# VectorE's order in a fused convolution and MLP kernel: taps moved behind one PSUM closing, another closing cut in two, one sum moved from GpSimd

## The chip, the core and the metric

The kernel runs on one core of a Trainium2 chip. The metric is the device time in microseconds (us) of one execution, the median of several. The engines of the core are called PE (TensorE: matrix products; PEld is its loading of weights, which overlaps the products), DVE (VectorE), ACT (ScalarE), POOL (GpSimd) and SP (SyncE, used here to start DMAs only). Each works through its own queue in the order in which the program was written, and waits on semaphores for what other engines and DMAs deliver.

## What is computed

The input `x` is 8 x 4224 x 192 floats. The reference does two things, one after the other:

```python
w = softmax(weight)                                   # 8 heads x 7 taps
out[b, s, c] = sum_k w[head(c), k] * x_pad[b, s + k, c]   # causal convolution along s
xn = (out - mean(out)) / sqrt(var(out) + 1e-6) * g_ln      # over the 192 channels
result = out + relu(xn @ w_ch1) @ w_ch2                    # 192 -> 768 -> 192
```

All of it is in float32. The convolved rows are called y below.

## The kernel before

**Tiling.** Rows are cut into 18 groups: three small ones at the start (g0 to g2), then g3 to g17 with 16 rows in each of the 128 partitions. Only the groups from g3 on, the "mixed" ones, matter here. The tiles are laid out by hand, the framework does no scheduling (`tc.manual_schedule()`), so the order of the statements is the order on each engine's queue; the framework adds only the waits.

**One group** goes through these stages. y is made by seven taps for each of 8 heads: tap 0 on ACT (`first_tap`, L384), tap 1 on ACT into a tile `tb` that a DMA started by POOL adds to y (`second_tap`, L395 and L398, "y<-tb"), and taps 2 to 6 on DVE (`conv`, L409, one instruction for a head and a tap). DVE then transposes y in 32x32 blocks to `yt` (L420). The up product is `up_mixed`, the down product `down_fast`. Both are one level of a seven-product block scheme (sums and differences of quarters replace the eighth product). For it, four sums of quarters of `yt`, called s1 to s4, are made by `sums_of_y` (L576 to L579): s1 = a21 + a22, s2 = s1 - a11, s3 = a21 - a11, and s4 in place of a21. The norm is folded in: its scale `rstd` multiplies the result at the end (`scale`, L886, on ACT), and the unscaled y was stored first, so that the scaled result is added to it in DRAM by a DMA (`add_to_out`, L893).

**The up product.** PSUM's eight banks make two sets, X (banks 0 to 3) and Y (banks 4 to 7). `up_mixed` has two passes, `one` and `two`, and each pass has seven products of about 2 us on PE (L519) that go to X and Y in turn. What a product leaves must be taken out before the set's next product but one starts: `evict` copies it with ACT (L617); `close` adds it to what is already there, with DVE (L623) where no spare tile is given, and with an ACT copy into a spare tile and a DMA accumulation (L582) where one is given. In every group but the last, DVE closes exactly two products, both of pass `two`: the **upper left** quarter `two.c11`, out of X after the second product, and the **lower left** quarter `two.c21`, out of X after the sixth. The product that follows the upper left closing in X is the fourth of the pass; what follows the lower left closing in X is the first down product, since `take_bank` hands out banks 0, 1, 2, ... from there. After a closing comes `lower_sum` (L773), a relu joined with a difference.

**The down product.** `down_fast` (L804) runs seven products of three column blocks each. The first one writes bank 0, 2 and 4 in this order. ACT takes each block out (L811) and between blocks does a few items of a list `work`: a relu of `one.c22`, scales of the group before, a relu of `two.c22`, and the first and second tap of the group after the next; `behind` says how many items go after each block. DVE does three sums over halves (`half_sum`, L771), adds to c11 (L836) and to a part (`add_part`, L853), starts the sums of y of the next group (L575 to L579) and takes the moments of its y (L440). DVE's `finish_fast` (L861: three transposes for each half, with an `add_part` ahead of the second half) is called from the next group's `up_mixed`, through the generator `ahead`.

**DVE's order around the change,** in one group: moments, `finish_fast` of the group before in two halves, 16 + 5 taps of the next group (taps 2 and 3, and tap 4 of five heads), upper left closing, 8 taps, `lower_sum` of pass one, lower left closing, `lower_sum` of pass two, 11 taps, transpose of the next y, the half sums.

**The last group** has no next group: DVE does all its closings itself, no taps stand between them, and the multiplication of the group before by `rstd` is done by DVE, in two instructions (L683), after the upper left closing of pass two.

Of the kernel before, what the change touches and what calls it, by code (L numbers as in the profile page):

```python
# [11 lines left out]
ALU = mybir.AluOpType  # L12
# [4 lines left out]
def kernel(  # L17
# [29 lines left out]
    nc = tc.nc  # L47
    PSUM = bass.MemoryType.PSUM
    B, S, D = x.shape
    H, K = weight.shape  # L50
    F = moe_w_ch1.shape[1]
    P = 128
# [10 lines left out]
    NQ = P // C  # L63
# [19 lines left out]
    HJ = J // 2  # L83
# [3 lines left out]
    W = HJ * C  # L87
# [285 lines left out]
    y, yt, rstd = {}, {}, {}  # L373
# [192 lines left out]
    def sums_of_y(g, engine):  # L566

        room = upool.tile([P, 3 * HJ * CH * C], F32, tag="ys", name=f"ysums{g}")
        room = room.rearrange("p (v j c t) -> p v j c t", v=3, c=CH, t=width(g))
        s1, s2, s3 = [room[:, v] for v in range(3)]  # L570
        a11, a12, a21, a22 = quarters_of_y(g)
        ysums[g] = s1, s2, s3, a21
        if engine is not nc.vector:

            nc.vector.memset(s1[:, 0:1, 0:1, 0:1], 0.0)  # L575
        engine.tensor_tensor(s1, a21, a22, op=ALU.add)  # L576
        engine.tensor_tensor(s2, s1, a11, op=ALU.subtract)
        engine.tensor_tensor(s3, a21, a11, op=ALU.subtract)
        engine.tensor_tensor(a21, a12, s2, op=ALU.subtract)  # L579
# [4 lines left out]
    def up_mixed(g, ahead, pending):  # L584


        last = g + 1 == NG
        assert groups[g][2] == 2 * HJ and 3 * W // 2 <= 512 and FC == PAIR + 1
        hidden_tile(g)
        a = ht[g]  # L590
        a11, a12, a21, a22 = quarters_of_y(g)
        b11, b12, b21, b22 = quarters_of_w1()
        t2, t3, t4 = [w1sums[:, k] for k in range(3)]
        s1, s2, s3, s4 = ysums[g]
        done = groups[g - 1][2]
        js = a11.shape[1] // 2

        class Pass:
            def __init__(self, s):
                self.s = s  # L600
                (self.c11, self.c12), (self.c21, self.c22) = [
                    [a[:, h, e, s] for e in range(2)] for h in range(2)
                ]

            def product(self, to, left, right, first=True, end=True):
                s = self.s
                for i, f, ps in (
                    (slice(0, W), s, slice(0, 2 * js)),
                    (slice(W, W + W // 2), PAIR, slice(js * s, js * s + js)),
                ):  # L610
                    rows_of_tiles(
                        to[:, :, i], right[:, :, P * f : P * f + P], left[:, ps], first and i.start == 0, end, True
                    )

            def evict(self, banks, dst, relu=False):
                src = banks[:, :, 0 : W + W // 2]
                nc.scalar.activation(dst, src, AF.Relu) if relu else nc.scalar.copy(dst, src)  # L617

            def close(self, c, banks, part=None):


                if part is None or last:
                    nc.vector.tensor_tensor(c, c, banks[:, :, 0 : W + W // 2], op=ALU.add)  # L623
                    return
                self.evict(banks, part)
                whole = "p q w -> p (q w)"
                add_by_dma(c.rearrange(whole), part.rearrange(whole))

            def relu(self, c):
                nc.scalar.activation(c, c, AF.Relu)  # L630

        def part_of(pool, tag):

            part = pool.tile([P, J * D], F32, tag=tag, name=f"part_{tag}{g}")
            return part[:, 0 : NQ * (W + W // 2)].rearrange("p (q w) -> p q w", q=NQ)

        def act_scales(j1, j2):
            if not last:
                scale(g - 1, j1, j2)

        def taps_of_next(*args, **kw):
            if not last:
                conv(g + 1, *args, **kw)


        X, Y = take_set(), take_set()
        one, two = Pass(0), Pass(1)
        p = one
        p.product(X, a11, b11, True, False)
        p.evict(X, p.c11)  # L650
        p.product(Y, a12, b21)
        p.close(p.c11, Y, two.c12)
        next(pending, None)
        p.product(X, s2, t2, False, False)
        p.evict(X, p.c21)
        p.product(Y, s3, t3, True, False)
        p.evict(Y, p.c22)
        next(ahead)
        p.product(X, s1, b12, False, False)
        p.close(p.c22, X, part_of(cpool, "cs"))  # L660
        next(pending, None)
        p.product(Y, a22, t4, False)
        p.close(p.c21, Y, part_of(bpool, "tb"))
        p.product(X, s4, b22, False)
        p.evict(X, p.c12, True)
        taps_of_next(2, 4)
        taps_of_next(4, 5, heads=(0, 5))

        p = two
        p.product(Y, a11, b11, True, False)  # L670
        p.evict(Y, p.c11)
        p.product(X, a12, b21)
        one.relu(one.c11)
        act_scales(0, 1)
        p.close(p.c11, X)
        taps_of_next(4, 5, heads=(5, H))
        taps_of_next(5, 6, heads=(0, 5))
        lower_sum(g, (0,))
        if last:

            for j1 in (0, HJ):
                part, factor = ots[g - 1][:, j1 : j1 + HJ], rstd[g - 1][:, j1 : j1 + HJ]
                nc.vector.tensor_tensor(  # L683
                    part, part, factor.unsqueeze(2).to_broadcast([P, HJ, D]), op=ALU.mult
                )
                add_to_out(g - 1, j1, j1 + HJ)
        p.product(Y, s2, t2, False, False)
        p.evict(Y, p.c21)
        p.product(X, s3, t3, True, False)
        p.evict(X, p.c22)  # L690
        p.product(Y, s1, b12, False, False)
        p.close(p.c22, Y, part_of(bpool, "tb"))
        p.product(X, a22, t4, False)
        p.relu(p.c11)
        act_scales(1, 2)
        p.close(p.c21, X)
        if last:
            one.relu(one.c22)
            p.relu(p.c22)
        p.product(Y, s4, b22, False)  # L700
        p.evict(Y, p.c12, True)
        lower_sum(g, (1,))
        if last:

            for f in range(FC):
                for s, ws, _ in columns(g, f, fast[g], J):
                    rest = a[:, 1, 0, s, :, ws]
                    nc.scalar.activation(rest, rest, AF.Relu)
        taps_of_next(5, 6, heads=(5, H))
        taps_of_next(6, K)  # L710

        def scale_one(j):
            scale(g - 1, j, j + 1)
            if j == 7:
                add_to_out(g - 1, 0, 8)
            elif j == done - 1:
                add_to_out(g - 1, 8, done)

        if last:
            return []  # L720
        work = [lambda: one.relu(one.c22)]
        work += [lambda j=j: scale_one(j) for j in range(2, done)]
        return work[0:9] + [lambda: two.relu(two.c22)] + work[9:]

    po = {}

# [124 lines left out]
    def add_part(half, cs, parts):  # L851
        fresh = cs[:, CH * half : CH * half + CH, 1]
        nc.vector.tensor_tensor(fresh, fresh, parts[half], op=ALU.add)  # L853

    def finish_fast(g, half, flat, cs, parts):
        n = fast[g]
        ot = ots[g] if half else out_tile(g)
        if half:
            add_part(half, cs, parts)
        for c in range(CH * half, CH * half + CH):  # L860
            nc.vector.transpose(  # L861
                ot[:, 0:n, C * c : C * c + C], flat[:, c].rearrange("p (j t) -> p j t", t=C)
            )
# [11 lines left out]
    ots = {}  # L875
# [12 lines left out]
    def add_to_out(g, j1, j2):  # L888
        if groups[g][0] is None:

            j1, j2 = (0, j2) if j2 == groups[g][2] else (0, 0)
        for ps, rows in rows_of_out(g, j1, j2) if j2 else ():
            nc.gpsimd.dma_start(  # L893
                out=rows, in_=ots[g][ps, j1:j2].rearrange("p j d -> p (j d)"), accum_op=ALU.add
            )
# [53 lines left out]
    results, pending = None, iter(())  # L949

    def ahead(g):


        if results is not None:
            for half in range(2):
                finish_fast(g - 1, half, *results)
        yield

    for g in range(NG):
        mixed, last = g in MIXED, g + 1 == NG  # L960
# [36 lines left out]
            store_y(g + 1)  # L997
        results = down_fast(g, work)
        if last:
            for half in range(2):  # L1000
                finish_fast(g, half, *results)
            add_and_store(g, slice(0, fast[g]))
            down(g)
            finish(g)
        else:
            if g % 2 or g + 2 == NG:
                pending = root(g + 1 - g % 2)
# [30 lines left out]
```

## Time and profile before

Three runs gave 981.8, 982.68 and 982.71 us; the median is 982.68 us. The profiled execution has a span of 980.9 us.

The groups show up as stretches between the first up product of one group and that of the next. A stretch holds the group's up product (14 products) and its down product. The starts come from PE's timeline:

| group | starts at us | length us | | group | starts at us | length us |
|---|---|---|---|---|---|---|
| g3 | 123.27 | 55.47 | | g11 | 574.67 | 58.21 |
| g4 | 178.74 | 55.48 | | g12 | 632.88 | 56.02 |
| g5 | 234.22 | 56.22 | | g13 | 688.90 | 55.63 |
| g6 | 290.44 | 58.28 | | g14 | 744.53 | 56.55 |
| g7 | 348.72 | 56.36 | | g15 | 801.08 | 57.22 |
| g8 | 405.08 | 56.20 | | g16 | 858.30 | 56.63 |
| g9 | 461.28 | 55.80 | | g17 | 914.93 | 66.0 to the end |
| g10 | 517.08 | 57.59 | | | | |

How to read the profile: a group of instructions is named by its line, its engine, its operation and "out<-in". In a timeline each line has the start, the duration, the engine, the line of code and, in square brackets, the idle time of that engine just before and what ended it. "issue" means that nothing in the profile explains the idle time. The down product took 27.4 to 27.5 us in each group from g3 to g16, so what varies in the table lies in the up products.

### The profile page before, as it was taken

Reading aid. Unit: us, or ns where it says so; the run is one execution under the profiler, and the core shown is the slowest. Engines: PE = TensorE matmul, PEld = TensorE weight load, DVE = VectorE, ACT = ScalarE, POOL = GpSimd, SP = SyncE. Lnnn points to the kernel's source line nnn. Section 1 sums busy time; section 2 is a strip of 40 time slices with the busy share of each in tenths; the row PEclk is TensorE's granted clock in tenths of the full one; section 3 lists DMA queues with packets and bytes.
Section 4 is the critical chain, followed back from the end, with each engine's and each line's share of the span. In section 5 each row is a group of like instructions: output and inputs, shape, how many; then the busy total and the mean of one; then the engine's idle time right before and its main releaser. Section 6 shows DMA issues by size and latency. Waiting matters only on the chain.

```text
span 980.9 us, 43680 instructions
## 1 busy us (share of the span) xinstructions
PE 956.8 (98%) x19962; PEld 748.5 (76%) x19962; DVE 906.8 (92%) x1439; ACT 667.2 (68%) x1069; POOL 293.7 (30%) x397
## 2 busy tenths in 40 slices
PE   6999999999999999999999999999999999999997
PEld 5886596877868686786959678695968778596887
DVE  6999999999998999999999899999999999999757
ACT  5625668586776968676786857678695867766351
POOL 2005311714144141534127141441317141261400
PEclk9999999999999999999999999999999999999999
DMA  8243887759495785949587684958868596755031
GB/s 197 96 132 122 178 196 202 156 128 254 100 269 114 214 188 123 240 99 278 119 236 155 157 206 95 276 119 238 165 171 199 101 269 123 182 113 99 3 67 68
DMA packets 24390, 158.14 MB, mean 161 GB/s; under 512 B 3343, under 2 KB 4239, under 8 KB 20110
## 3 DMA queue, kind: packets, MB, share of 16 engines
q0 software_dynamic: 17104, 92.02, 47.9%
q1 hardware_dynamic: 6798, 63.34, 17.5%
q8 instruction: 156, 2.56, 1.0%
q14 instruction: 28, 0.23, 0.1%
q10 hardware_dynamic: 304, 0.00, 0.0%
HBM read 38.95 MB, written 50.33 MB: 91 GB/s over the span
## 4 chain that ended last, share of the span: by engine, by line
PE 71%; ACT 10%; DMA 9%; DVE 8%; issue 2%; POOL 1%; SPq 0%; DVEq 0%; ACTq 0%; POOLq 0%
PE ps L519 36%; PE ps L804 28%; DMA y<-tb 6%; PE ps L745 6%; DVE y L409 6%; ACT ot L886 3%; ACT y L384 2%; ACT tb L395 2%; ACT room L630 1%; ACT cs L811 1%; DVE room L623 1%; DMA xg<-in_x_dram 1%; DMA room<-part_tb 1%; PE ps L321 1%; DMA ga<-in_moe_g_ln_dram 1%
## 5 line engine op out<-in xcount | busy, mean ns | idle before, releaser
L409 DVE SCALAR_TENSOR_TENSOR y<-xg,taps,y 128x384 f32<-128x384 f32 (+3 forms) x734 | 368.7, 579 | 11.7 <-issue 10.7
L519 PE MATMUL ps<-yt,w 32*128 32x256 f32 (+3 forms) x5184 | 239.0, 334 | 4.3 <-issue 3.0
L519 PEld LDWEIGHTS ps<-yt,w 32*128 32x128 f32 x5184 | 220.7, 186 | 23.5 <-issue 11.6
L804 PE MATMUL ps<-room,w2sums 128*32 128x256 f32 (+3 forms) x4416 | 236.5, 371 | 1.4 <-issue 1.4
L617 ACT COPY room<-ps 128x1536 f32<-128x1536 f32 x104 | 149.7, 1439 | 90.4 <-PE ps L519 90.4
L804 PEld LDWEIGHTS ps<-room,w2sums 128*32 128x32 f32 x4416 | 140.7, 110 | 91.7 <-ACT room L630 5.4
L804 PE MATMUL ps<-room,w 128*32 128x256 f32 (+3 forms) x3312 | 180.7, 371 | 0.2 <-issue 0.2
L771 DVE TENSOR_TENSOR room<-room 128x1536 f32<-128x1536 f32 (+1 forms) x96 | 149.0, 1622 | 16.6 <-ACT cs L811 9.7
L804 PEld LDWEIGHTS ps<-room,w 128*32 128x32 f32 x3312 | 104.8, 110 | 65.8 <-DVE room L623 1.8
L519 PE MATMUL ps<-ysums,w1sums 32*128 32x128 f32 (+1 forms) x2880 | 130.1, 325 | 3.8 <-DVE room L623 2.1
L519 PEld LDWEIGHTS ps<-ysums,w1sums 32*128 32x128 f32 x2880 | 120.9, 186 | 10.4 <-DVE room L623 4.1
L811 ACT COPY cs<-ps 128x256 f32<-128x256 f32 (+1 forms) x180 | 65.3, 364 | 47.3 <-PE ps L804 46.9
L886 ACT ACTIVATE ot<-ot,r 128x192 f32<-128x192 f32 x232 | 94.1, 453 | 0.0
L893 POOL DMA_DIRECT2D out_dram<-ot x40 | 34.3, 1087 | 187.5 <-ACT ot L886 160.2
L630 ACT ACTIVATE room<-room 128x1536 f32<-128x1536 f32 x60 | 89.2, 1490 | 0.0
L623 DVE TENSOR_TENSOR room<-room,ps 128x1536 f32<-128x1536 f32 x34 | 59.5, 1752 | 22.4 <-PE ps L519 22.0
L384 ACT ACTIVATE y<-xg,taps 128x384 f32<-128x384 f32 (+3 forms) x141 | 74.0, 604 | 8.5 <-DMA out_dram<-y 6.9
L440 DVE BATCH_NORM_STATS2 st<-y 128x6 f32<-128x192 f32 x264 | 70.3, 348 | 0.0
L582 POOL DMA_DIRECT2D room<-part_tb x28 | 24.2, 865 | 149.2 <-DVE room L773 102.5
L519 PE MATMUL ps<-yt,w1sums 32*128 32x256 f32 (+1 forms) x1440 | 66.3, 323 | 1.2 <-issue 1.2
L519 PE MATMUL ps<-ysums,w 32*128 32x256 f32 (+1 forms) x1440 | 65.9, 323 | 0.6 <-issue 0.6
L811 ACT COPY room<-ps 128x256 f32<-128x256 f32 (+1 forms) x90 | 32.1, 375 | 49.3 <-PE ps L804 49.3
(106 smaller groups left out, 980.4 us busy)
## 6 DMA issues: line engine op xcount, KB each, us to landing
xg<-in_x_dram SPq DMA_DIRECT2D x15, 2112.0 KB, 19.8
out_dram<-ot POOLq DMA_DIRECT2D x29, 768.0 KB, 9.8
y<-tb POOLq DMA_DIRECT2D x28, 768.0 KB, 11.4
room<-part_tb POOLq DMA_DIRECT2D x28, 768.0 KB, 6.3
out_dram<-y SPq DMA_DIRECT2D x13, 1536.0 KB, 10.8
room<-room POOLq DMA_DIRECT2D x14, 768.0 KB, 6.3
room<-part_cs POOLq DMA_DIRECT2D x14, 768.0 KB, 6.3
xg<-in_x_dram SPq DMA_DIRECT2D x1, 1536.0 KB, 7.5
```

What stands on the lines that cost most here:

```text
L384: nc.scalar.mul(y[g][:, 0:n, cs], xg[g][:, 0:n, cs], taps[:, h, 0:1])
L409: nc.vector.scalar_tensor_tensor(out=y[g][:, 0:n, cs], in0=t[:, k : k + n, cs], scalar=taps[:, h, k : k + 1], in1=y[g][:, 0:n, cs], op0=AL ...
L440: nc.vector.bn_stats(out=sums[g][:, j, :], in_=y[g][:, j, :])
L519: nc.tensor.matmul(to[:, q], right[rows, c], left[rows, :, c], skip_group_check=split, start=(first and c == 0), stop=(last and c == left. ...
L617: nc.scalar.activation(dst, src, AF.Relu) if relu else nc.scalar.copy(dst, src)
L623: nc.vector.tensor_tensor(c, c, banks[:, :, 0 : W + W // 2], op=ALU.add)
L630: nc.scalar.activation(c, c, AF.Relu)
L745: nc.tensor.matmul(bank[C * q : C * q + C, 0:w], w2[:, f, C * c : C * c + C], left, start=(f == 0), stop=(f == NF - 1),)
L771: nc.vector.tensor_tensor(d, l, r, op=op)
L804: nc.tensor.matmul(dst[C * q : C * q + C, ws], right[:, f, C * c : C * c + C], view[:, :, q] if len(view.shape) == 4 else view[:, q], star ...
L811: nc.scalar.copy(out[:, c], dst[:, 0:w].rearrange("p (j t) -> p j t", t=t))
L886: nc.scalar.mul(ots[g][:, j, :], ots[g][:, j, :], rstd[g][:, j : j + 1])
```

## The change

It rearranges DVE's queue, with a few moves that go with it:

1. **Fewer taps ahead of the upper left closing.** Of tap 4's five heads that stood ahead of it, three go behind it, so that 18 taps stand ahead and 11 behind, where 21 and 8 stood.
2. **Lower left closing in two pieces.** `close` gets `pieces`; the closing of `two.c21` becomes two instructions, for banks 0 and 1 and for banks 2 and 3. It comes later in the queue by the three taps, and the first piece alone frees the bank that the down product wants first.
3. **First sum of y on DVE.** s1 is made by DVE instead of POOL. A small memset on DVE that held POOL's first sum back until DVE was there goes away.
4. **The relu of `two.c22` in two instructions** on ACT, the columns that are needed first ahead. The list `work` gets one item longer.
5. **`finish_fast` in two steps.** The generator `ahead` yields after the first half and `add_part`; `up_mixed` takes this first step ahead of the closing of `one.c11`. Except in the last group, DVE has no instruction in between, so its order stays.
6. **The last group's output work forward.** The two multiplications by `rstd` and their DMAs go ahead of pass two, from behind its upper left closing.

The diff, cut to its core:

```diff
@@ sums_of_y
-        if engine is not nc.vector:
-            nc.vector.memset(s1[:, 0:1, 0:1, 0:1], 0.0)
-        engine.tensor_tensor(s1, a21, a22, op=ALU.add)
+        nc.vector.tensor_tensor(s1, a21, a22, op=ALU.add)
         engine.tensor_tensor(s2, s1, a11, op=ALU.subtract)
@@ Pass.close
-            def close(self, c, banks, part=None):
+            def close(self, c, banks, part=None, pieces=1):
                 if part is None or last:
-                    nc.vector.tensor_tensor(c, c, banks[:, :, 0 : W + W // 2], op=ALU.add)
+                    for i in range(pieces):
+                        qs = slice(NQ * i // pieces, NQ * (i + 1) // pieces)
+                        nc.vector.tensor_tensor(
+                            c[:, qs], c[:, qs], banks[:, qs, 0 : W + W // 2], op=ALU.add
+                        )
                     return
@@ up_mixed, pass one
         p.product(Y, a12, b21)
+        next(ahead)
         p.close(p.c11, Y, two.c12)
...
         taps_of_next(2, 4)
-        taps_of_next(4, 5, heads=(0, 5))
+        taps_of_next(4, 5, heads=(0, 2))
+
+        if last:
+            for j1 in (0, HJ):
+                part, factor = ots[g - 1][:, j1 : j1 + HJ], rstd[g - 1][:, j1 : j1 + HJ]
+                nc.vector.tensor_tensor(
+                    part, part, factor.unsqueeze(2).to_broadcast([P, HJ, D]), op=ALU.mult
+                )
+                add_to_out(g - 1, j1, j1 + HJ)
@@ up_mixed, pass two
         p.close(p.c11, X)
-        taps_of_next(4, 5, heads=(5, H))
+        taps_of_next(4, 5, heads=(2, H))
         taps_of_next(5, 6, heads=(0, 5))
         lower_sum(g, (0,))
-        if last:
-            for j1 in (0, HJ):
-                part, factor = ots[g - 1][:, j1 : j1 + HJ], rstd[g - 1][:, j1 : j1 + HJ]
-                nc.vector.tensor_tensor(
-                    part, part, factor.unsqueeze(2).to_broadcast([P, HJ, D]), op=ALU.mult
-                )
-                add_to_out(g - 1, j1, j1 + HJ)
...
-        p.close(p.c21, X)
+        p.close(p.c21, X, pieces=2)
@@ the list work
-        return work[0:9] + [lambda: two.relu(two.c22)] + work[9:]
+        halves = [lambda ws=ws: two.relu(two.c22[:, :, ws]) for ws in (slice(W, W + W // 2), slice(0, W))]
+        return work[0:9] + halves + work[9:]
@@ ahead
-            for half in range(2):
-                finish_fast(g - 1, half, *results)
+            flat, cs, parts = results
+            finish_fast(g - 1, 0, flat, cs)
+            add_part(1, cs, parts)
+        yield
+        if results is not None:
+            finish_fast(g - 1, 1, flat, cs)
         yield
```

More of the change, by code (lines that the diff above doesn't have):

```diff
@@ L853, in add_part, with finish_fast @@
         nc.vector.tensor_tensor(fresh, fresh, parts[half], op=ALU.add)
-    def finish_fast(g, half, flat, cs, parts):
+    def finish_fast(g, half, flat, cs):
         n = fast[g]
         ot = ots[g] if half else out_tile(g)
-        if half:
-            add_part(half, cs, parts)
         for c in range(CH * half, CH * half + CH):
@@ L999 @@
         if last:
-            for half in range(2):
-                finish_fast(g, half, *results)
+            flat, cs, parts = results
+            finish_fast(g, 0, flat, cs)
+            add_part(1, cs, parts)
+            finish_fast(g, 1, flat, cs)
             add_and_store(g, slice(0, fast[g]))
```

## The prediction

> **What bounds the kernel.** The page's busy line comes first, then the busy time of each engine by group:
>
> ```profile
> PE 956.8 (98%) x19962; PEld 748.5 (76%) x19962; DVE 906.8 (92%) x1439; ACT 667.2 (68%) x1069; POOL 293.7 (30%) x397
> 178.70:234.20 55.50, 55.50 (x1180) 43.12 (x1176) 53.89 (x80) 41.98 (x66) 23.69 (x33) 1.00 0.70 173
> 290.40:348.70 58.30, 56.72 (x1180) 44.27 (x1176) 53.88 (x80) 41.97 (x66) 22.75 (x33) 1.00 0.72 175
> 348.70:405.10 56.40, 55.54 (x1184) 43.05 (x1180) 53.80 (x81) 41.97 (x66) 14.24 (x13) 1.00 0.75 181
> ```
>
> The last three are g4, g6 and g7: stretch and length, then PE, PEld, DVE, ACT, POOL. PE runs almost without a pause in a good group, so 55.47 us (g3, g4) is nearly PE's own time. DVE has 53.8 us of work in each, 1.7 us less: it is a near second. Over g3 to g16 the lengths exceed 55.47 us by 791.66 - 14 x 55.47 = 15.1 us; that, small gaps inside the good groups and the last group are all that can be gained.
>
> The waits of PE, asked for group by group, split those 15.1 us in two. In g7, g8, g9, g12 and g13 PE waits for DVE's closing, or for nothing that is shown in g3 and g4; their excess is 0.89 + 0.73 + 0.33 + 0.55 + 0.16 = 2.66 us. In g5, g6, g10, g11, g14 and g15 the waits say "issue", in pieces of 0.3 to 0.9 us, between 13 and 26 us after the group's start; excess 0.75 + 2.81 + 2.12 + 2.74 + 1.08 + 1.75 = 11.25 us. g16 has 1.16 us, mostly a wait for ACT behind a DMA. Here is the first kind, DVE and PE in g7:
>
> ```profile
> 367.70 1.75 DVE L623 TENSOR_TENSOR room<-room,ps 128x1536 f32<-128x1536 f32 x1
> 369.37 4.32 DVE L409 SCALAR_TENSOR_TENSOR y<-xg,taps,y 128x384 f32<-128x384 f32 x8
> 373.60 1.76 DVE L773 SCALAR_TENSOR_TENSOR room<-room 128x1536 f32<-128x1536 f32 x1
> 375.82 1.75 DVE L623 TENSOR_TENSOR room<-room,ps 128x1536 f32<-128x1536 f32 x1 [0.47 <-PE ps L519]
> ...
> 369.51 2.24 PE L519 MATMUL ps<-ysums,w1sums 32*128 32x256 f32 x48 [0.86 <-DVE room L623]
> 377.63 4.09 PE L804 MATMUL ps<-room,w 128*32 128x256 f32 x72
> ```
>
> The upper left closing starts at 367.70 straight after the taps, late; PE idles 0.86 us for it. The lower left one waits for PE, so there DVE has time to spare. The chain of waits tells why the first is late:
>
> ```profile
> 379.57 1.39 ACT room L630
> ...
> 397.96 0.54 POOL y L398
> 398.50 12.60 DMA y<-tb
> ...
> 412.78 10.35 DVE y L409 x20
> ...
> 423.99 1.68 DVE room L623
> ```
>
> It is a ring from closing to closing: down product 9.93 us after the closing; ACT's list of relus, scales and taps; the DMA that adds the second tap to y; taps at 412.78, which is 35.15 us after that down product began (377.63); 11.2 us of taps; closing. 9.93 + 35.15 + 11.2 = 56.28 us, and the closings 367.70 and 423.99 are 56.29 us apart. The ring is 0.8 us longer than PE's group. g3 and g4 had slack in hand; from g7 on it sets the pace wherever no "issue" pause has given slack back.
>
> **What the Trainium skill says.** "SBUF — State Buffer", section "SBUF: two separate sides": a DVE instruction with two SBUF inputs and a GpSimd instruction that reads SBUF exclude each other for a whole instruction. The trace agrees: `add_part` takes 0.95 us when POOL is idle, 2.54 us at 292.52, while POOL's last sum runs until 294.25. "Perfetto Trace Analysis", section "Optimizing Scalar/DVE Operations": some 60 ns on SBUF and 125 ns on PSUM are paid for each DVE instruction, and breaking an instruction up can free others sooner. "Runtime: NRT & Kernel Launch", section "Instruction fetch mechanics": instructions come by DMA in blocks of 256. The page has 156 such packets (2.56 MB, 16 KB each); the "issue" pauses of g6 lie 6.1 and 6.2 us apart, and 256 of PE's instructions, half of them products of which 48 go in 1.96 us, are 128 / 48 x 1.96 = 5.2 us, or about 5.9 with a pause of 0.6. So I take those pauses for fetches, an inference. The edits leave PE's instructions alone, so I leave the 11 us.
>
> **The change, part by part.** T is the start of the upper left closing.
>
> *Three taps behind it.* A tap costs 11.2 / 21 = 0.534 us in a row, so DVE comes to the closing 1.6 us earlier. The ring falls to 56.28 - 1.6 = 54.7 us. PE then sets T.
>
> *What they delay.* In g7 DVE goes from 367.70 through closing, 8 taps and `lower_sum` to 375.28, T + 7.58; with three more taps T + 9.18. The lower left closing, which before started when PE was done, now starts when DVE is. Where PE sets T (g4: T = 196.85, the product in X ended near 196.5, the next one needs T + 1.8) the four products after it end at T + 9.76, and the down product began at T + 9.93. Now the first piece decides. The price of a piece has no row: 0.951 us is DVE's own 128x768 sum in SBUF, and between 417 ns for 128x256 out of PSUM (L836) and 1752 ns for 128x1536 (L623) a straight line gives 0.95 for 768 as well; with the page's larger PSUM share 1.0. I take 0.95: piece one ends at T + 10.13, PE begins 0.07 later (the step from 369.45 to 369.51 in g7) at T + 10.2. That is 0.27 us worse than before in a group where PE sets T. The second piece ends at T + 11.05, and the bank it frees is wanted one block after T + 10.2, a third of 3.9 us later: T + 11.5, hidden. Without pieces it would be T + 11.0: they are needed.
>
> Queued behind are `lower_sum` (wanted 3.9 us after the down product began: T + 14.1, it ends T + 12.8, hidden), 11 taps, transpose, then the half sums: they waited 0.52 us for PE and now come some 0.2 us late, with their first use 3.9 us after they start. Hidden.
>
> *The relu in two.* PEld waits 0.4 us for it (ACT L630) in every group, and the second and third down products take 7.88 us where two others take 7.77. The first piece comes half a us sooner: -0.11 us a group. On the ring it costs one more ACT instruction, 0.1 us, and the list is one longer (33 items, 30 go in the first four products, two after the next block), so the last second tap goes behind one more copy, 0.27 us: +0.37 us. Ring: 54.7 + 0.27 + 0.37 = 55.3 us, under PE's group.
>
> *PE's group now:* 55.47 + 0.27 - 0.11 = 55.63 us where PE sets T. In the groups with a pause between T and the down product (g5, g6, g10, g11, g14, g15, g16) DVE has that pause in hand (T + 9.76 plus 0.6 or more), so the pieces remove even the 0.17 us gap: -0.17 - 0.11 = -0.28, of which I take 0.25.
>
> *First sum on DVE.* It adds 0.95 us and takes away 0.06; POOL's three sums end 1.0 us sooner (it began 0.2 us after the memset, now after the sum: 0.95 + 0.2 + 3 x 1.83 against 0.2 + 4 x 1.83), so `add_part`, which lost 1.6 us to the lock, loses none. DVE gains 0.7 us, and its taps wait for the DMA anyway (1.09 us idle before them in the chain). Zero. *`finish_fast` in two:* zero, order unchanged but for g17, where DVE had waited 3.98 us.
>
> *Last group.* 3.42 us of multiplication go into a wait of 4.55 us of DVE ahead of 933.71. The closing of c22 can then start with PE at 939.7, not 940.12; PE had lost 0.42 us there and 0.2 at the down product. Gain 0.5 us. The tail from 966 on is PE and its last output, untouched.
>
> **Sum.** g3, g4, g7, g8, g9, g12, g13: 7 x 0.16 = 1.1 us of excess instead of 2.66, -1.55. Seven groups with a pause: -7 x 0.25 = -1.75. Last group -0.5. Together -3.8: **978.9 us**.
>
> **Rivals.** *A, the lower left closing becomes the bound.* The down product waits for both pieces, or pieces cost well over 1 us. For it: the closing loses its whole slack of 0.47 us, and DVE is 97% busy. Against: each piece has banks of its own. Then PE begins at T + 9.18 + 1.9 + 0.07 = T + 11.15, 1.2 us later than before: 7 x 1.1 - 2.66 for the quiet groups, some 7 x 0.3 for the others, -0.5 at the end: +6.6, 989 us. *B, one wait for another.* The ring goes but each piece costs 0.2 us more than I think, or the DMA of the second tap, issued 0.37 us later, lands later by 1 us. Then 14 x 0.25 = 3.5 of my gain is eaten: 982.4 us. *C, the pauses shrink.* With ring and gaps gone the engines stand otherwise to the DMAs; a third of the 11.25 us of pauses goes: 975.2 us. The same could go the other way; nothing in the profile says which.
>
> **Chances.** Forecast 0.54, A 0.13, B 0.18, C 0.15. The range goes from a little under C to beyond B, with half of the way to A left out: 974.5 to 984.0. Faster by more than 0.2% (under 980.7): the forecast less one in ten, and C: 0.65. Slower (over 984.6): A and a little of the pauses growing: 0.16. The rest, 0.19, lies within.
>
> **What would show it.** In a quiet group (g4, g8): the idle time of PE before its fourth product of pass two ("DVE room L623") at 0.3 us or none, closings 55.6 us apart, DVE idle ahead of the upper left closing for PE, none ahead of the lower left one; a first piece of 0.95 us ending 10.1 us after T and the down product at once; no PEld wait for L630; `add_part` at 0.95 us each time; "issue" pauses in the same groups. I am wrong if the down product starts later than T + 10.5, if the taps still begin so late that PE waits, or if the pauses move.

## The result and the profile after

The changed kernel takes 977.27 us (median of 4 runs, 974.48 to 978.25) where the kernel before takes 982.69; the ratio is 0.9942, 95% interval 0.992 to 0.9965. That is 5.4 us or 0.55% faster. The profiled executions have spans of 974.4 and 980.9 us, 6.5 us apart.

The busy line of the page of the changed kernel, and the busy time of each engine in g4, g6 and g7 (stretch and length, PE, PEld, DVE, ACT, POOL):

```profile
PE 952.9 (98%) x19962; PEld 746.3 (77%) x19962; DVE 897.1 (92%) x1454; ACT 668.4 (69%) x1083; POOL 266.6 (27%) x383
179.40:235.00 55.60, 55.38 (x1180) 43.06 (x1180) 52.98 (x81) 42.06 (x67) 21.37 (x32) 1.00 0.70 172
290.60:348.50 57.90, 56.34 (x1177) 43.90 (x1177) 53.41 (x82) 42.06 (x67) 21.42 (x32) 1.00 0.73 176
348.50:404.20 55.70, 55.48 (x1184) 43.17 (x1180) 52.73 (x80) 42.06 (x67) 12.12 (x12) 1.00 0.76 184
```

g4 and g7 are now alike at 55.6 us, and DVE has about a microsecond less to do in each; g6 is still the long one. The chain that ended last, from the page before and then from the page after, says the same for the whole kernel:

```profile
PE 71%; ACT 10%; DMA 9%; DVE 8%; issue 2%; POOL 1%; SPq 0%; DVEq 0%; ACTq 0%; POOLq 0%
```

```profile
PE 86%; DVE 8%; DMA 2%; issue 2%; POOL 1%; ACT 0%; DVEq 0%; POOLq 0%; ACTq 0%
```

ACT and the DMA of the second tap have left it: the ring from closing to closing no longer sets the pace. Summed over the kernel, PE waited 2.4 us before for DVE's closings inside the up products and shows no such wait after; at the down products it now waits 1.7 us for them, eight times. What took its place stands in the timeline of DVE and PE in g7 of the changed kernel (lines are numbered anew: the closings are L622, `lower_sum` L777, the down product L808):

```profile
356.21 9.62 DVE L409 SCALAR_TENSOR_TENSOR y<-xg,taps,y 128x384 f32<-128x384 f32 x18 [1.84 <-issue]
366.60 1.75 DVE L622 TENSOR_TENSOR room<-room,ps 128x1536 f32<-128x1536 f32 x1 [0.77 <-PE ps L519]
368.27 5.91 DVE L409 SCALAR_TENSOR_TENSOR y<-xg,taps,y 128x384 f32<-128x384 f32 x11
374.09 1.75 DVE L777 SCALAR_TENSOR_TENSOR room<-room 128x1536 f32<-128x1536 f32 x1
375.76 1.81 DVE L622 TENSOR_TENSOR room<-room,ps 128x768 f32<-128x768 f32 x2
...
366.28 4.37 PE L519 MATMUL ps<-ysums,w1sums 32*128 32x256 f32 x96
376.76 4.09 PE L808 MATMUL ps<-room,w 128*32 128x256 f32 x72 [0.21 <-DVE room L622]
```

The wait has changed sides. DVE now stands idle for 0.77 us ahead of the upper left closing, PE has no marked wait there (its two products from 366.28 on run as one row of 4.37 us), and the lower left closing, which had waited 0.47 us for PE, now starts straight after `lower_sum`; PE waits 0.21 us for its first piece.

The lengths by group in us, from PE's timeline:

| group | before | after | change | | group | before | after | change |
|---|---|---|---|---|---|---|---|---|
| g3 | 55.47 | 55.60 | +0.13 | | g10 | 57.59 | 57.19 | -0.40 |
| g4 | 55.48 | 55.60 | +0.12 | | g11 | 58.21 | 58.16 | -0.05 |
| g5 | 56.22 | 55.62 | -0.60 | | g12 | 56.02 | 55.78 | -0.24 |
| g6 | 58.28 | 57.97 | -0.31 | | g13 | 55.63 | 55.60 | -0.03 |
| g7 | 56.36 | 55.60 | -0.76 | | g14 | 56.55 | 56.55 | 0.00 |
| g8 | 56.20 | 55.60 | -0.60 | | g15 | 57.22 | 57.07 | -0.15 |
| g9 | 55.80 | 55.59 | -0.21 | | g16 | 56.63 | 55.88 | -0.75 |

g3 to g16 together: 791.66 before, 787.81 after, -3.85 us. The last group: from 65.97 us (980.9 - 914.93) to 62.88 us (974.4 - 911.52), -3.09 us. What comes before g3 is 0.44 us longer (123.71 against 123.27); another profile of the same changed kernel begins g3 at 126.66, so that part varies by itself. -3.85 - 3.09 + 0.44 = -6.5.

### The profile page after: what moved, and what is told of

It reads as the page before. It is cut to its first block, busy times and chain, and to the rows that moved or that the text cites. A ratio compares the mean times of both kernels' runs of the same rounds, so it can differ in the third digit from the quotient of the medians.

```text
span 974.4 us, 43710 instructions
## 1 busy us (share of the span) xinstructions
PE 952.9 (98%) x19962; PEld 746.3 (77%) x19962; DVE 897.1 (92%) x1454; ACT 668.4 (69%) x1083; POOL 266.6 (27%) x383
## 4 chain that ended last, share of the span: by engine, by line
PE 86%; DVE 8%; DMA 2%; issue 2%; POOL 1%; ACT 0%; DVEq 0%; POOLq 0%; ACTq 0%
PE ps L808 41%; PE ps L519 38%; PE ps L749 6%; DVE y L409 5%; DVE room L622 2%; DMA xg<-in_x_dram 1%; DMA room<-part_tb 1%; PE ps L321 1%; DMA ga<-in_moe_g_ln_dram 1%; DVE room L777 0%; PE ps L345 0%; PE ps L350 0%; POOL room L579 0%; POOL d L452 0%; DVE y L902 0%
## 5 line engine op out<-in xcount | busy, mean ns | idle before, releaser
L808 PE MATMUL ps<-room,w2sums 128*32 128x256 f32 (+3 forms) x4416 | 233.9, 370 | 0.0
L808 PEld LDWEIGHTS ps<-room,w2sums 128*32 128x32 f32 x4416 | 140.9, 110 | 87.4
L808 PE MATMUL ps<-room,w 128*32 128x256 f32 (+3 forms) x3312 | 179.9, 370 | 1.7 <-DVE room L622 1.7
L808 PEld LDWEIGHTS ps<-room,w 128*32 128x32 f32 x3312 | 104.1, 110 | 67.2 <-DVE room L622 3.2
L631 ACT ACTIVATE room<-room 128x1536 f32<-128x1536 f32 (+2 forms) x74 | 90.5, 1245 | 0.0
L622 DVE TENSOR_TENSOR room<-room,ps 128x768 f32<-128x768 f32 (+1 forms) x49 | 60.5, 1261 | 29.2 <-PE ps L519 28.9
```

The lines of the kernel that those rows point to most:

```text
L622: nc.vector.tensor_tensor(c[:, qs], c[:, qs], banks[:, qs, 0 : W + W // 2], op=ALU.add)
L808: nc.tensor.matmul(dst[C * q : C * q + C, ws], right[:, f, C * c : C * c + C], view[:, :, q] if len(view.shape) == 4 else view[:, q], star ...
```

## The experiments

Each was compared with the kernel before on its own chip. There that kernel took 984.8 to 985.4 us, so ratios are compared, and the changed kernel was run again on the chip of shift, s1pool and relu1 (`again`). Beside the ratio stands the sum of g3 to g16 from the run's profile, one profile for each run.

| run | what it is | ratio to before (95%) | g3 to g16, us | quiet group, us |
|---|---|---|---|---|
| first run | changed kernel | 0.9942 (0.992 to 0.9965) | 787.81 | 55.60 |
| again | changed kernel | 0.994 (0.9922 to 0.9957) | 788.25 | 55.60 |
| taps21 | three taps back | 0.9961 (0.9949 to 0.9973) | 791.18 | 55.3 to 56.6 |
| piece1 | closing in one | 1.0013 (1.0004 to 1.0023) | 796.23 | 56.40 |
| lastback | last group's work back | 0.9955 (0.9938 to 0.9972) | 791.33 | 55.60 |
| taps19 | one tap back | 0.9942 (0.9921 to 0.9964) | 786.51 | 55.3 to 55.7 |
| s1pool | first sum on POOL | 0.9937 (0.9918 to 0.9957) | 788.23 | 55.60 |
| relu1 | relu in one | 0.9952 (0.9934 to 0.997) | 789.08 | 55.71 |
| shift | 52 more PE instructions | 0.9968 (0.9958 to 0.9979) | 789.34 | 55.60 |
| b_last | before, last group's work forward | 0.9981 (0.997 to 0.9993) | 791.63 | 55.5 to 56.3 |
| taps19b3 | one tap back, DMA sooner | 0.9917 (0.9893 to 0.9941) | 787.11 | 55.3 to 55.7 |

Runs of one kernel spread by several microseconds (taps19: 976.13 to 987.29), so intervals are 0.1 to 0.25% to either side and the traces have to carry the finer statements. A single trace has its own chance in it: b_last, whose g3 to g16 are those of the kernel before, gives the same sum (791.63 against 791.66) but 55.74 us for g7 where that has 56.36, and lastback, whose g3 to g16 are those of the changed kernel, is 3.5 us above it through pauses in one group.

**again.**

> The changed kernel itself once more, beside the others on the same chip, so that their profiles and times have one to stand against. Quiet groups 55.6 us, down products 27.33 us, the last group 62.9 us from its first product to the end; 0.994 of the kernel before.

As expected: quiet groups 55.60, down products 27.33, the last group 62.9 us (977.8 - 914.91), ratio 0.994. The length of g11 differs by 0.44 us (58.60 against 58.16) with the same program.

**taps21: are the three taps a gain or only a trade?**

```diff
-        taps_of_next(4, 5, heads=(0, 2))
+        taps_of_next(4, 5, heads=(0, 5))
...
-        taps_of_next(4, 5, heads=(2, H))
+        taps_of_next(4, 5, heads=(5, H))
```

> The changed kernel (977.3 us) with the three taps put back ahead of the upper left closing (21 ahead, 8 behind), all else as changed. Trade theory (the ring is real, but what the taps cost ahead of one closing they cost ahead of the other): the down product begins 9.8 us after the upper left closing instead of 10.16, and the ring from closing to closing is 9.8 + 35.0 + 11.2 = 56.0 us, against 55.6 now. g3 and g4 take 55.25 us, from some group on 55.9 to 56.0; PE waits up to 0.8 us for the upper left closing and no longer at the down product. Sum of about -0.4 x 2 + 0.3 x 3 and little for the others: 977 to 978.5 us. Rival (the three taps are the main gain): the quiet groups go back to what they were before, some 1.6 us or more in all, and further 0.4 us for each group of the longer list of work: 979 to 981 us.

My trade theory fell on the trace: the groups are 3.4 us longer in sum (791.18 against 787.81), 2.2 us of it in the seven quiet ones, and PE waits 3.9 us in all for DVE's closings inside the up products, where the changed kernel has no such wait. The times alone would not tell: the ratio is 0.9961, and its interval overlaps that of the changed kernel. The ring is back in full, as the timeline of DVE in g7 and g8 of this run and PE's wait in g7 show:

```profile
358.02 11.21 DVE L409 SCALAR_TENSOR_TENSOR y<-xg,taps,y 128x384 f32<-128x384 f32 x21 [1.98 <-issue]
369.14 1.75 DVE L622 TENSOR_TENSOR room<-room,ps 128x1536 f32<-128x1536 f32 x1
...
377.22 1.82 DVE L622 TENSOR_TENSOR room<-room,ps 128x768 f32<-128x768 f32 x2 [0.43 <-PE ps L519]
...
414.15 1.15 DVE L409 SCALAR_TENSOR_TENSOR y<-xg,taps,y 128x384 f32<-128x384 f32 x2 [1.95 <-issue]
...
370.94 2.25 PE L519 MATMUL ps<-ysums,w1sums 32*128 32x256 f32 x48 [0.84 <-DVE room L622]
```

Taps follow the DMA after an idle 2 us, the closing follows the taps with no gap, the second closing waits for PE again. From taps to taps it is 414.15 - 358.02 = 56.13 us, and g7 and g8 take 56.17 and 56.13 us. I had put the ring at 56.0 and counted it in three groups only; it slowed g5 and g9 as well (56.24 and 56.58 us).

**piece1: what are the two pieces worth?**

```diff
-        p.close(p.c21, X, pieces=2)
+        p.close(p.c21, X)
```

> The changed kernel with the lower left closing in one instruction again (128x1536), so that the down product has to wait for all of it. Theory that the closing is on PE's path in each quiet group: the down product begins at T + 9.18 + 1.75 + 0.07 = T + 11.0 us instead of T + 10.16; PE's wait at its first product goes from 0.2 to 1.1 us in g3, g4, g5, g7, g8, g9, g12, g13 (8 x 0.85 = 6.8 us) and some 0.3 us in the groups whose pause hides a part: 984 to 986 us. Rival (the first piece is no better than the whole, since the product waits for both pieces): no change, 977 us.

The quiet groups take 56.40 us, 0.80 more than with two pieces, and the sum is 8.4 us longer. DVE and PE in this run's g7:

```profile
372.17 1.75 DVE L622 TENSOR_TENSOR room<-room,ps 128x1536 f32<-128x1536 f32 x1 [0.75 <-PE ps L519]
...
381.33 1.75 DVE L622 TENSOR_TENSOR room<-room,ps 128x1536 f32<-128x1536 f32 x1
...
383.13 4.09 PE L808 MATMUL ps<-room,w 128*32 128x256 f32 x72 [1.01 <-DVE room L622]
```

The down product begins 383.13 - 372.17 = 10.96 us after the upper left closing, where two pieces give 10.16; over the kernel PE waits 9.3 us there instead of 1.7. This kernel is slower than the one before (by 0.13%, interval 0.04 to 0.23%), though it has all the other parts: moving the taps without cutting the closing loses more than it gains.

**taps19: is one of three taps too many behind?**

```diff
-        taps_of_next(4, 5, heads=(0, 2))
+        taps_of_next(4, 5, heads=(0, 3))
...
-        taps_of_next(4, 5, heads=(2, H))
+        taps_of_next(4, 5, heads=(3, H))
```

> The changed kernel with one tap of the three back ahead of the upper left closing (19 ahead, 10 behind). DVE now stands idle for 0.7 us ahead of that closing, more than a tap (0.53 us), while PE waits 0.2 us behind the other. Trade theory: the upper left closing stays where PE sets it, the down product begins at T + 9.8 instead of T + 10.16, a quiet group takes 55.25 instead of 55.6 us: 8 x 0.35 = 2.8 us, 974.5 us. Rival (the ring is longer than I think: the slack of 0.7 us goes, since the groups get shorter too): the groups stay at 55.5 to 55.6 us, 977 us.

Half of it came. g4, g7 and g13 take 55.3 us as forecast; g5, g8, g9 and g12 take 55.5, and g3 55.67. In g8 DVE has next to nothing left in hand: the taps begin after 1.96 us of waiting and the closing follows them with 0.04 us of idle time, as the first two of these lines of g8 show (0.05 us in g7, 0.15 in g9).

```profile
412.52 10.14 DVE L409 SCALAR_TENSOR_TENSOR y<-xg,taps,y 128x384 f32<-128x384 f32 x19 [1.96 <-issue]
422.71 1.75 DVE L622 TENSOR_TENSOR room<-room,ps 128x1536 f32<-128x1536 f32 x1
...
429.10 1.44 ACT L614 COPY part_tb<-ps 128x1536 f32<-128x1536 f32 x1 [0.83 <-DMA room<-part_tb]
```

So the ring is about as long as the group, which is the rival's reason. But it is not what costs these groups their 0.2 us: the fourth product of pass two, the one behind the closing, starts 19.91 us after the group's start in g8 and g9 as in g4 and g7, which take 55.3 us. g8 loses its 0.17 us at the last product of the pass, which comes late behind ACT's copy at 429.10, and that waited 0.83 us for a DMA. In g12 DVE still waits 0.37 us for PE, and PE had lost 0.12 us ahead of that closing already. The sum is 1.3 us below the changed kernel's, and the times tell no difference.

**taps19b3: can the ring be shortened?**

```diff
-        product(0, a[:, 1, 1], w2sums[:, 1], parts[0], False, 2)
+        product(0, a[:, 1, 1], w2sums[:, 1], parts[0], False, 3)
```

(on top of taps19)

> 19 taps ahead of the upper left closing, and three items of the list instead of two after the first block of the fifth down product, so that the last second tap does not go behind one more copy and its DMA is issued 0.3 us sooner. Theory: with 19 taps the down product begins when PE is ready, and the ring (55.5 us in some groups of that kernel) falls to 55.2: all eight quiet groups at 55.3 us, some 1 us less than with 19 taps alone and 2.5 us less than the changed kernel: 0.991 to 0.992 of the kernel before. Rival (the DMA's landing does not follow its issue, or the pauses grow): quiet groups still 55.5 us, 0.994.

It bought nothing that the trace shows: g5, g8 and g9 still take 55.67, 55.59 and 55.43 us, the taps of g8 still begin after 2.03 us of waiting, and the sum is 787.11 us, no better than with 19 taps alone. The ratio, 0.9917, is the lowest of all, but its interval reaches those of taps19 and of the changed kernel; whether it beats them stays open.

**lastback and b_last: the last group's output work.** Undone in the changed kernel, and done alone in the kernel before; each moves this block from one place to the other:

```diff
         if last:
             for j1 in (0, HJ):
...
                 nc.vector.tensor_tensor(
                     part, part, factor.unsqueeze(2).to_broadcast([P, HJ, D]), op=ALU.mult
                 )
                 add_to_out(g - 1, j1, j1 + HJ)
```

> The changed kernel with the last group's two multiplications and their DMAs put back behind the upper left closing of pass two. Theory that the two DMAs to DRAM ran into PE's instruction fetch in the last down product: they start again some 11 us later, the last group's down product, 19.1 us from its first product to the last stage, shows pauses marked issue again (2.9 us together) and takes about 22 us: 977.3 + 2.9 + 0.3 for the closing = 980.2 us to 980.6. Rival (only DVE's 3.4 us of multiplication counted, as I forecast): the closing of c22 is 0.4 us late, no pauses, 977.8 us.

> The kernel before with part 6 alone: the last group's two multiplications and their DMAs ahead of pass two. Theory of the collision: the last group, 66.0 us from its first product to the end, loses the pauses marked issue of its down product (2.9 us) and 0.2 to 0.3 us of a late closing: 62.8 to 63.0 us, and the kernel before minus 3.1 us, 0.997 of it. Groups g3 to g16 as before. Rival (only the closing): 65.6 us, 0.9995 of the kernel before.

Both agree with the collision and not with my forecast of 0.5 us. With the work late the last group takes 65.97 us (before) and 65.98 us (lastback, 984.3 - 918.32); with the work early 62.88 us (after) and 62.91 us (b_last, 981.5 - 918.59). The ratios of b_last (0.9981) and lastback (0.9955) point the same way, though to some 1.9 and 1.4 us and not to 3.1, with wide intervals. The 791.33 us that g3 to g16 take in lastback hold three pauses in g7 (0.47, 1.41 and 0.72 us; the group takes 59.22 us), where its edit changes nothing, and the profiled execution is the slowest of its seven.

The busy share of the DMA engines in the last group, 40 slices of 1.65 us from 915 on before, and 40 of 1.56 us from 911.5 on after:

```profile
DMA  0000000000000009999940000000000000780070
```

```profile
DMA  0000000000098999700000000000000000690052
```

Before, the DMAs are full in slices 15 to 19, 939.8 to 948.0 us, and half busy to 949.7; after, from 928.7 to 938.1 us. PE's last down product begins at 944.10 before and at 940.46 after. PE's timeline, before and then after:

```profile
944.10 2.91 PE L804 MATMUL ps<-room,w 128*32 128x176 f32 x96
946.83 0.46 PE L804 MATMUL ps<-room,w2sums 128*32 128x176 f32 x2
948.66 5.60 PE L804 MATMUL ps<-room,w2sums 128*32 128x176 f32 x187 [1.37 <-issue]
```

```profile
940.46 2.91 PE L808 MATMUL ps<-room,w 128*32 128x176 f32 x96
943.18 5.58 PE L808 MATMUL ps<-room,w2sums 128*32 128x176 f32 x192
```

The product that met the busy DMAs stops for 1.37 us with no releaser named; once the DMAs have ended ahead of it, it runs through. From first to last of these seven products it is 21.95 us before (944.10 to 966.05) and 19.1 after (940.46 to 959.56). The 1.37 us and four shorter stops make up the 2.85 us between them; the five stand 256 of PE's instructions apart (see the last section), the later four after the DMAs had ended. In lastback the pause is there again, 1.39 us; in b_last there is none.

**shift: are the pauses fetches of instructions?**

```diff
         for _ in range(times):
             nc.tensor.matmul(idle[:, 0:P], less, copy, start=True, stop=True)
+        for _ in range(13):
+            nc.tensor.matmul(idle[:, 0:8], less, copy[:, 0:8], start=True, stop=True)
```

> The changed kernel with 13 narrow matrix products (128x8, their result is never read) added to the warm-up at the start: 52 more instructions for PE, which is what a group of 2352 or some more is beyond nine blocks of 256. Fetch theory: a pause comes where a block boundary of PE's instruction stream meets a busy stretch of DMA, so each group now stands where the next one stood, and the pauses marked issue leave g6, g11 and g15 and come to g4, g5, g9, g10, g13 or g14 (g5 and g10 keep some, larger ones in g5 and g10 than in g6 and g11). The sum stays at some 8 to 11 us, the time within 2 us of the changed kernel. Rival (the pauses are set by what the DMAs or DVE do in these groups, for instance the alternation of the root's work or the batch): they stay in g6, g10, g11, g14 and g15.

The main pauses moved one group ahead. The first two of g6 in the changed kernel, whose g6 begins at 290.53, and the first two of g5 in this run, whose g5 begins at 236.85:

```profile
304.69 4.76 PE L519 MATMUL ps<-yt,w 32*128 32x128 f32 x115 [0.60 <-issue]
310.62 3.54 PE L519 MATMUL ps<-ysums,w1sums 32*128 32x256 f32 x81 [0.34 <-issue]
```

```profile
251.04 4.75 PE L521 MATMUL ps<-yt,w 32*128 32x128 f32 x114 [0.52 <-issue]
256.96 3.54 PE L521 MATMUL ps<-ysums,w1sums 32*128 32x256 f32 x81 [0.35 <-issue]
```

They lie 14.16 and 20.09 us after the start of the one, 14.19 and 20.11 us after the start of the other. g6, g11 and g15 are quiet now (55.60, 55.68 and 55.60 us), g5, g10 and g14 are the long ones (57.03, 58.26 and 58.06 us). Nothing but the place of the instructions in PE's stream differs in these groups, so the pauses belong to positions in that stream. g7 has a new pause (0.67 us, the group takes 56.71), at the same place in a block of instructions as the others (see the last section). Not all is explained: g16 waits 2.2 us for ACT behind a DMA (57.81 us), and 0.9968 is worse than the changed kernel's 0.994, though the profile is no longer than that of `again` (978.0 against 977.8 us).

**s1pool: the first sum on POOL again.**

```diff
-        nc.vector.tensor_tensor(s1, a21, a22, op=ALU.add)
+        if engine is not nc.vector:
+            nc.vector.memset(s1[:, 0:1, 0:1, 0:1], 0.0)
+        engine.tensor_tensor(s1, a21, a22, op=ALU.add)
```

> The changed kernel with the first sum of y back on POOL behind the small memset of DVE. Theory that DVE waits for the DMA of the second tap anyway: the second add_part takes 2.5 us again, DVE's idle time ahead of the taps (1.6 to 2.2 us, issue) falls by 0.7 us, the closings and PE stay where they are: quiet groups 55.6 us, the same time within 1 us. Rival (DVE's order is what sets the taps): quiet groups 0.5 us or more longer, 5 us or more in all.

As the theory says. In g7 of this run `add_part` takes 2.20 us instead of 0.92 (the first line is from the changed kernel, the others from this run), DVE's idle time ahead of the taps is 1.38 us instead of 1.84, and nothing on PE's path moves:

```profile
351.45 0.92 DVE L857 TENSOR_TENSOR cs<-cs,room 128x768 f32<-128x768 f32 x1
...
352.17 2.20 DVE L859 TENSOR_TENSOR cs<-cs,room 128x768 f32<-128x768 f32 x1
...
357.75 9.61 DVE L409 SCALAR_TENSOR_TENSOR y<-xg,taps,y 128x384 f32<-128x384 f32 x18 [1.38 <-issue]
```

Ratio 0.9937 and quiet groups of 55.60: this part of the change is worth nothing in time here.

**relu1: the relu of `two.c22` in one.**

```diff
-        halves = [lambda ws=ws: two.relu(two.c22[:, :, ws]) for ws in (slice(W, W + W // 2), slice(0, W))]
+        halves = [lambda: two.relu(two.c22)]
```

> The changed kernel with the relu of two.c22 in one instruction again, the list one item shorter. Theory: the third down product waits 0.11 us for it in each of 14 groups, down products take 27.44 instead of 27.33 us, nothing else changes on PE's path: 1.5 us longer. The DMA of the second tap lands 0.3 to 0.4 us sooner, which gives DVE more idle time ahead of the upper left closing and no time. Rival (the shorter list counts, since the ring is close): the same time or less.

The down products take 27.44 to 27.45 us again instead of 27.33, in every group, and up products of the quiet groups stay at 28.27: 14 x 0.115 = 1.6 us. The times agree in direction only (0.9952 against 0.994, intervals that overlap).

## Why the prediction was right, and where it was not

*The bound and the two kinds of excess:* right. PE at about 55.5 us a group, a ring from closing to closing a little longer, pauses of its own. taps21 shows the ring returning with the three taps, shift that the pauses belong to PE's instruction stream, and the DMA records that they wait for fetches (last section). One reading was off: the two distances between the pauses of g6 are 5.9 and 6.2 us (304.77, 310.70, 316.89), not 6.1 and 6.2; the estimate of 5.9 us fits still.

*Three taps behind, closing in two pieces:* right in mechanism, and in each number but one. The down product was to begin at T + 10.2 and began at 376.76 - 366.60 = T + 10.16; one piece was to take 0.95 us and takes 0.948 in the mean (two in a row 1.81); quiet groups were to take 55.63 and take 55.60. Their sum (g3, g4, g7, g8, g9, g12, g13) was to fall by 1.55 and fell by 1.59 us; so close a fit is partly luck, since b_last has these seven groups 0.3 us shorter than the kernel before with the same instructions. The number that was off is the ring: it was to be 55.3 us, but DVE's 0.69 and 0.83 us of idle time ahead of the closing in g8 and g9 leave 54.9 and 54.8, so the 0.37 us put down to the longer list did not show. What rival A feared is what piece1 brings about, with the delay given for it: T + 10.96 where the rival had T + 11.15, and g3 to g16 4.6 us above the kernel before where it had 7.1. With two pieces it did not come.

*Relu in two:* right, 0.11 us a group. *First sum and `finish_fast`:* zero, as said. DVE's idle time for the DMA hides the first (s1pool); the terms given for POOL's sums make 0.9 us and not 1.0, which changes nothing. `finish_fast` was not tried alone, but the last group, the only one in which it changes DVE's order, takes 62.91 us without it (b_last) and 62.88 with it.

*Groups with a pause:* -1.75 forecast, -2.26 measured, but not as forecast, a quarter of a microsecond each: g5 -0.60 and g16 -0.75, g11 and g14 nearly nothing. Two profiles of the same kernel differ by up to 0.44 us in one of these groups, so the single figures carry little. Rival C, pauses that shrink, did not come here: those marked issue sum to 6.30 us before and 5.96 after in g3 to g16. It came in the last group.

*The last group* is the term that was mis-sized: -0.5 forecast, -3.09 measured. The step said that DVE's multiplication goes into a wait and that "the tail from 966 on is PE and its last output, untouched". It counted the closing and the down product behind it as 0.6 us of lost time, where PE gained 0.23 us (up product 29.17 to 28.94 us), and overlooked the DMAs that the moved instructions release. They had been at work into the first products of the last down product. The pause of 1.37 us stood in the profile before, next to a DMA issue at 940.51, and I had left all pauses alone because PE's instructions don't change. The other side of the collision, the time of the DMAs, did change.

The forecast of 978.9 us was 1.6 us above the 977.27 measured, less than the 2.6 us of that term: the traces fell by 6.5 us, the medians by 5.4. The total lay in the range because the range was wide enough for a term that the forecast did not see.

## What to carry to other kernels

When work is moved from ahead of one deadline to ahead of the next, work out the second deadline as well: here moving three taps gains 3.4 us of the traced groups when the closing behind them is cut in two (taps21 against the changed kernel), and with that closing whole the kernel is slower than it was (piece1). A producer that must release several buffers can release first the one that is wanted first, in a piece that costs 0.06 us more in all (1.81 against 1.75). And an instruction that starts a transfer is moved together with its transfer: ask what else will use the DMA engines then, the instruction fetch of the busiest engine included.

## What was not expected of the hardware

PE stops for want of instructions in a program without branches: pauses of 0.1 to 1.4 us, at fixed positions in its stream, some 9 us in 974 after the change (what g6, g10, g11, g14 and g15 take beyond 55.6 us). The Trainium skill, "Runtime: NRT & Kernel Launch", section "Instruction fetch mechanics", calls the cost of a block boundary mostly hidden; here it is hidden while the DMA engines are quiet (the last down product after the change has no pause), and not while accumulations to DRAM of 768 KB each fill them (the same product before, where four more blocks came late after the DMAs had ended).

The DMA records of the traces match single fetches to the pauses. The twelve profiles have 150 pauses of PE of more than 0.1 us marked issue in the up and down products. Counted over PE's records, products and weight loads, all of them stand whole multiples of 256 instructions apart (at 193 or 194 beyond a multiple), and each ends 2.2 to 2.6 us after a 16 KB packet of the instruction queue began. In the changed kernel the packets ahead of its eleven pauses began 3.5 to 4.5 us after PE had passed the place 256 instructions earlier, and the other queues kept the DMA engines at least 86% busy in between; for the rest of its packets the median is 1.3 us. This also accounts for why the pauses in the middle of the kernel come in the up products alone: 256 instructions take 5.4 us there in the median of the changed kernel and 6.7 to 6.9 us in the down products of these groups, where no packet began more than 3.7 us behind that place, soon enough by these figures. Why the profile of one execution has pauses in a group in which the next has none (g7 of lastback), and why the kernel before takes 982.7 us on one chip and 985 on others, stays open.
